# A column of 128 maxima is turned by a second VectorE transpose and stored as four rows of 32

## The chip, the cores and the metric

The kernel runs on one core of a Trainium2 chip. The metric is the device time of one execution in microseconds (us), taken as the median over several executions. The engines are named as the profile names them: PE is TensorE's matmul (PEld its weight load), DVE is VectorE, ACT is ScalarE, POOL is GpSimd, and SPq is the queue of SyncE, from which nearly all transfers are issued.

## The reference

Two branches of the same input x (2048 rows of 512) are computed and mixed by a gate. Branch a is attention with 32 query heads of width 16 that share one key head and one value head; branch b is a feed-forward layer with SiLU. Everything is float32.

```python
def _A_ref(x, wq, wk, wv, wo):
    q = (x @ wq).reshape(B, S, H, Dh).transpose(0, 2, 1, 3)   # H = 32, Dh = 16
    k = x @ wk
    v = x @ wv
    scores = jnp.einsum("bhqd,bkd->bhqk", q, k) * (Dh ** -0.5)
    p = softmax(scores, axis=-1)
    o = jnp.einsum("bhqk,bkd->bhqd", p, v)
    return o.transpose(0, 2, 1, 3).reshape(B, S, H * Dh) @ wo
def _B_ref(x, w1, w2):
    h = silu(jnp.einsum("bsd,df->bsf", x, w1))                # 512 -> 1792
    return jnp.einsum("bsf,fd->bsd", h, w2)                   # 1792 -> 512
g = sigmoid((x * gate_w).sum(-1, keepdims=True))
out = g * _A_ref(x, wq, wk, wv, wo) + (1 - g) * _B_ref(x, w1, w2)
```

## The kernel before

Operands are split into two float16 parts with fixed scales, and each product is made of three float16 matmuls. The fixed scales hold only while the data lie in certain ranges. The kernel therefore works in two passes. The first pass computes the whole output with fixed scales and, on the side, collects maxima of its operands. At its end line 1461 reads `flag`, and a second pass with scales worked out from the data runs only if a maximum lay outside its range (`RANGES`).

After a short prologue the first pass is one long pipeline, `attention`. It goes through 32 rounds, one for each block of 512 query rows, block of 128 query columns (8 heads) and half of these heads. A round has 16 steps, one for each 128 keys. In a step PE writes scores into a PSUM tile `S` (line 1212, in eight matmuls of 32 rows), ACT turns them into exponentials `P` (line 1218, 128x1024 at a time, two of them a step), DVE takes the lower half of `P`'s mantissa into a float16 tile `L` (line 1237), and PE adds value sums from `P` and `L` (line 1316). Between these, PE does the matmuls of the feed-forward layer, of the next queries and of the output projection (line 869). At the end of a round DVE takes the sums out of PSUM by two transposes (lines 1137 and 1138), and POOL and DVE finish them.

The instructions of each engine stand in an order that a planner in the kernel wrote out when it was built. It keeps its own estimates of when each engine is free (`pe`, `act`, `dve`, `pool`), and counts PE's instructions in blocks of 256, of which each takes at least `BLOCK` = 3.65 us by its estimate. On the chip each engine keeps to its order and waits for semaphores.

SPq's queue is in order as well. At the start of each round `load_q` (lines 268 to 272) issues eight loads from DRAM into the query buffer `qb` that the next round uses, in rows of 1 KB. They wait until PE is through with the last use of that buffer.

The collected maxima are small DVE work, the `chores`, which the planner puts where it believes DVE to be free. Each `absmax` leaves a column of `mxs` (128 x 32). Once all query blocks are done, `gather` runs: it adds the last column (lines 694 and 695), turns `mxs` in blocks of 32 x 32 (line 696, the result in `mt`, columns 0 to 31 of the buffer `raw`), takes the maximum of each row (line 697, into `mr`, column 32 of the same buffer) and stores the 128 maxima into a small DRAM tile `md` (line 698). `row` loads `md` back as one row on one partition (line 703), `check` compares it with `RANGES` (lines 709 to 714), and `verdict` writes `flag` (lines 717 to 719).

Of the kernel before, what the change touches and what calls it, by code (L numbers as in the profile page):

```python
# [47 lines left out]
def kernel(  # L48
# [21 lines left out]
    nc = tc.nc  # L70
# [35 lines left out]
    raw_ = [consts.tile([128, 512], F32, name=f"raw{n}") for n in range(2)]  # L106
# [7 lines left out]
    md = dram.tile([128], F32, name="md")  # L114
# [21 lines left out]
    def absmax(dst, src, axis=AX.X):  # L136
        nc.vector.tensor_reduce(dst, src, axis=axis, op=OP.max, apply_absolute_value=True)
# [539 lines left out]
    def chores():  # L677

        todo = []
        for kt in range(KD):  # L680
            for h in range(2):
                todo.append(lambda kt=kt, h=h: absmax(mxs[:, M_X + 2 * kt + h:M_X + 2 * kt + h + 1], xs[:, 0, kt, h * S // 2:(h + 1) * S // 2]))
                todo.append(lambda kt=kt, h=h: absmax(mxs[:, M_1 + 2 * kt + h:M_1 + 2 * kt + h + 1], w1s[:, 0, kt, h * F // 2:(h + 1) * F // 2]))
        for f in range(0, FT_ALL, 2):
            todo.append(lambda f=f: absmax(mxs[:, M_2 + f // 2:M_2 + f // 2 + 1], flat(w2s[:, 0, f:f + 2])))
        for o in range(0, NO, 2):
            todo.append(lambda o=o: absmax(mxs[:, M_O + o // 2:M_O + o // 2 + 1], flat(wo_s[:, 0, o:o + 2])))

        todo.append(lambda: absmax(mxs[:, M_Q:M_Q + 1], flat(wqs[:, 0])))
        todo.append(lambda: absmax(mxs[:, M_VV:M_VV + 1], VF[:, :, 0:16], AX.XY))  # L690

        def gather():
            mt, mr = raw_[0][:, 0:32], raw_[0][:, 32:33]
            nc.vector.tensor_reduce(mr[0:64], um, axis=AX.X, op=OP.min)
            nc.vector.tensor_scalar(mxs[0:64, M_B:M_B + 1], mr[0:64], -1.0, SHIFT * LAM / ONE, op0=OP.mult, op1=OP.add)
            nc.vector.transpose(mt, mxs)
            nc.vector.tensor_reduce(mr, mt, axis=AX.X, op=OP.max)
            nc.sync.dma_start(md.rearrange("(p o) -> p o", o=1), mr)

        m, m1 = raw_[1][0:1, 0:128], raw_[1][0:1, 128:160]  # L700

        def row():
            nc.sync.dma_start(m, md.rearrange("(o p) -> o p", o=1))

        g = raw_[1][0:1, 160:160 + 4 * len(RANGES)].rearrange("p (a b) -> p a b", a=4)

        def check(n0):
            if n0 == 0:
                nc.vector.tensor_reduce(m1, m.rearrange("p (a b) -> p b a", a=4), axis=AX.X, op=OP.max)
            for n in range(n0, min(n0 + 3, len(RANGES))):  # L710
                a, b, lo, hi = RANGES[n]
                nc.vector.tensor_reduce(g[:, 0, n:n + 1], m1[:, a:b], axis=AX.X, op=OP.max)
                nc.vector.tensor_scalar(g[:, 1, n:n + 1], g[:, 0, n:n + 1], lo, None, op0=OP.is_lt)
                nc.vector.tensor_scalar(g[:, 2, n:n + 1], g[:, 0, n:n + 1], hi, None, op0=OP.is_gt)

        def verdict():
            nc.vector.tensor_tensor(g[:, 3], g[:, 1], g[:, 2], op=OP.max)
            nc.vector.tensor_reduce(g[:, 0, 0:1], g[:, 3], axis=AX.X, op=OP.max)
            nc.vector.tensor_copy(flag, g[:, 0, 0:1])

        return todo, gather, row, *(lambda n=n: check(n) for n in range(0, len(RANGES), 3)), verdict


# [767 lines left out]
```

## Time and profile before

| | us |
|---|---|
| median of three executions | 1073.58 (1071.99 to 1075.55) |
| the profiled execution, its own time | 1073.73 |
| its span, first to last instruction | 1071.9 |
| the time around the span | 1.8 |
| `md` is stored (SPq, line 698) at | 753.64 |
| `md` is loaded back (SPq, line 703) at | 762.71 |

In what follows a row of the groups reads: line, engine, operation, what it writes and reads, how many, busy time. A row of the timeline reads: start in the span, duration, engine and operation, how many were merged, and in square brackets the engine's idle time before it with what ended that. A row of the waits reads: who waited for whom, time in total, how many times, the longest. A row of the stages reads: the stretch, its length, busy time and number of instructions of PE, PEld, DVE, ACT and POOL, then the clock that TensorE was granted as a share of the full one, the share of the 16 DMA engines that was busy, and GB/s.

### The profile page before, as it was taken

Reading aid. Unit: us, or ns where it says so; the run is one execution under the profiler, and the core shown is the slowest. Engines: PE = TensorE matmul, PEld = TensorE weight load, DVE = VectorE, ACT = ScalarE, POOL = GpSimd, SP = SyncE. Lnnn points to the kernel's source line nnn. Section 1 sums busy time; section 2 is a strip of 40 time slices with the busy share of each in tenths; the row PEclk is TensorE's granted clock in tenths of the full one; section 3 lists DMA queues with packets and bytes.
Section 4 is the critical chain, followed back from the end, with each engine's and each line's share of the span. In section 5 each row is a group of like instructions: output and inputs, shape, how many; then the busy total and the mean of one; then the engine's idle time right before and its main releaser. Section 6 shows DMA issues by size and latency. Waiting matters only on the chain.

```text
span 1071.9 us, 65095 instructions
## 1 busy us (share of the span) xinstructions
PE 1019.1 (95%) x30622; PEld 565.9 (53%) x30622; DVE 909.3 (85%) x823; ACT 1000.5 (93%) x1116; POOL 470.9 (44%) x396
## 2 busy tenths in 40 slices
PE   8999999899999999999999999999899999999997
PEld 5445555455555555555555555555445555545553
DVE  6699889999999778888887888888788798888886
ACT  6899999999999999999999999999899999999990
POOL 2035326634252464344742436266344266644641
PEclk9999999999999999999999999999999999999999
DMA  7321111100000100000000010000000000000001
GB/s 255 89 66 56 55 56 55 31 11 22 12 21 15 40 22 12 22 12 21 5 22 12 12 60 12 21 6 21 12 11 11 10 26 31 12 11 12 4 4 43
DMA packets 23783, 32.90 MB, mean 31 GB/s; under 512 B 5121, under 2 KB 13474, under 8 KB 23506
## 3 DMA queue, kind: packets, MB, share of 16 engines
q1 hardware_dynamic: 22978, 28.49, 8.5%
q8 instruction: 241, 3.95, 1.5%
q14 instruction: 36, 0.29, 0.1%
q0 software_dynamic: 96, 0.10, 0.0%
q10 hardware_dynamic: 432, 0.07, 0.0%
HBM read 20.12 MB, written 8.52 MB: 27 GB/s over the span
## 4 chain that ended last, share of the span: by engine, by line
PE 37%; DVE 23%; ACT 22%; issue 8%; POOL 8%; DMA 1%; SPq 0%; DVEq 0%; ACTq 0%; POOLq 0%
ACT P L1218 20%; DVE L L1237 14%; PE pm L869 13%; PE pv L1316 12%; PE S L1212 8%; POOL T L1143 2%; ACT e L883 2%; POOL U L1145 2%; POOL U L1150 2%; PE S L873 1%; POOL T L1146 1%; PE pm L873 1%; DVE e L888 1%; DVE U L1138 1%; DVE w2s L203 1%
## 5 line engine op out<-in xcount | busy, mean ns | idle before, releaser
L1218 ACT ACTIVATE P<-S 128x1024 f32<-128x1024 f32 x1024 | 963.2, 1070 | 32.3 <-PE S L1212 27.7
L1237 DVE TENSOR_TENSOR L<-P 128x2048 f16<-128x2048 f32 x240 | 599.3, 2514 | 27.7 <-ACT P L1218 27.0
L1212 PE MATMUL S<-qb,KT 50*32 50x512 f16 x8192 | 438.1, 380 | 13.8 <-ACT P L1218 11.3
L1212 PEld LDWEIGHTS <-KT 50*32 50x32 f16 x8192 | 188.8, 90 | 232.1 <-issue 149.7
L1316 PE MATMUL pv<-P,VF 64*32 64x512 f32 (+1 forms) x5552 | 306.6, 499 | 0.0
L869 PE MATMUL pm<-w2s,H 64*32 64x512 f16 x4800 | 255.0, 377 | 4.7 <-issue 2.7
L869 PE MATMUL pm<-xs,w1s 64*32 64x512 f16 x5376 | 254.4, 376 | 4.7 <-DVE e L888 3.4
L1143 POOL TENSOR_TENSOR T<-T,U 128x512 f32<-128x512 f32 x31 | 84.5, 2725 | 287.1 <-DVE U L1138 287.1
L890 POOL CAST H<-e 128x512 f16<-128x512 f32 x56 | 54.4, 971 | 215.5 <-DVE e L888 215.5
L869 PEld LDWEIGHTS <-w1s 64*32 64x32 f16 x5376 | 109.0, 93 | 60.5 <-issue 17.8
L869 PEld LDWEIGHTS <-H 64*32 64x32 f16 x4800 | 108.5, 93 | 49.9 <-issue 9.8
L1316 PEld LDWEIGHTS pv<-P,VF 64*32 64x32 f32 x5552 | 109.2, 106 | 39.7 <-issue 7.4
L1316 PE MATMUL pv<-L,VP 64*32 64x512 f16 x1904 | 102.6, 377 | 10.4 <-DVE L L1237 10.1
L1316 PE MATMUL pv<-P,VP 64*32 64x512 bf16 x1904 | 106.5, 388 | 1.4 <-DVE T L1137 0.9
L891 POOL TENSOR_TENSOR H<-e,H 128x512 f16<-128x512 f32 x56 | 103.6, 1850 | 4.5
L1316 PEld LDWEIGHTS <-VP 64*32 64x32 f16 x3808 | 69.1, 93 | 56.4 <-issue 31.5
L869 PE MATMUL pm<-xs,wqs 64*32 64x512 f16 x1152 | 85.0, 375 | 0.8 <-DVE e L888 0.6
L888 DVE SCALAR_TENSOR_TENSOR e<-e,pm 128x512 f32<-128x512 f32 x56 | 38.1, 681 | 42.3 <-ACT e L883 42.3
L1150 POOL TENSOR_TENSOR U<-U 128x48 f32<-128x48 f32 (+1 forms) x62 | 69.8, 1126 | 2.4
L869 PE MATMUL pm<-wo_s,O 64*32 64x512 f16 x1440 | 67.5, 375 | 1.2 <-DVE acc L843 0.8
L1145 POOL TENSOR_TENSOR U<-T,mu 128x96 f32<-128x96 f32 x31 | 47.6, 1535 | 2.4
L843 DVE SCALAR_TENSOR_TENSOR acc<-pm,g,acc 128x512 f32<-128x512 f32 x42 | 31.3, 745 | 16.1 <-PE pm L869 15.3
(180 smaller groups left out, 608.0 us busy)
## 6 DMA issues: line engine op xcount, KB each, us to landing
qb<-qd SPq DMA_DIRECT2D x189, 32.0 KB
raw<-in_B_w_dram SPq DMA_DIRECT2D x22, 256.0 KB
xn<-in_A_x_dram SPq DMA_DIRECT2D x8, 512.0 KB
out_dram<-acc SPq DMA_DIRECT2D x16, 256.0 KB
qd<-qx SPq DMA_DIRECT2D x12, 256.0 KB
w1r<-in_B_w_dram SPq DMA_DIRECT2D x2, 512.0 KB
raw<-in_A_wo_dram SPq DMA_DIRECT2D x4, 256.0 KB
qb<-sh SPq DMA_DIRECT2D x62, 2.0 KB
```

Of the source, the lines that this page charges most:

```text
L843: nc.vector.scalar_tensor_tensor(a, po, gate[:, n:n + 1], a, op0=OP.mult, op1=OP.add)
L869: nc.tensor.matmul(self.bank[32 * m:32 * m + 32], l(i, rows, 32 * m), r(j, rows), start=first, stop=last)
L888: nc.vector.scalar_tensor_tensor(e, e, 1.0, ph, op0=OP.add, op1=OP.mult)
L890: nc.gpsimd.tensor_copy(H[:, 0], e)
L891: nc.gpsimd.tensor_tensor(H[:, 1], e, H[:, 0], op=OP.subtract)
L1143: eng.tensor_tensor(T, T, U, op=OP.add)
L1145: eng.tensor_tensor(z[:, :, 1:1 + DIGITS], T3[:, :, 17:17 + DIGITS], mu[:, :, 1:].to_broadcast([128, 16, DIGITS]), op=OP.mult)
L1150: eng.tensor_tensor(first, first, second, op=OP.add)
L1212: nc.tensor.matmul(sc[32 * m:32 * m + 32, f], KT[b:b + 50, k0:k0 + 32], qtile[i][b:b + 50, j], start=True, stop=True)
L1218: nc.scalar.activation(P[:, 2 * j:2 * j + 2], sc, AF.Exp, scale=scale_of(c, o))
L1237: nc.vector.tensor_tensor(L[s], P, upper(P), op=OP.subtract)
L1316: nc.tensor.matmul(pvs[i][h][32 * j:32 * j + 32, cols], a[r], b[r, j, cols], start=start, stop=rest == n)
```

## The change

In `gather` the maxima stand in column 32 of `raw`, one on each of 128 partitions. After the change a second DVE transpose reads columns 32 to 63 of `raw` and writes columns 0 to 31. It turns each block of 32 x 32, so the 32 maxima of partitions 0 to 31 become row 0 of the result, those of 32 to 63 row 32, and so on; the other rows hold what lay in columns 33 to 63 and are not used. The store takes rows 0, 32, 64 and 96, 32 values each, instead of 128 single values. The bytes in `md` are the same, and so is all that reads them.

```diff
             nc.vector.transpose(mt, mxs)
             nc.vector.tensor_reduce(mr, mt, axis=AX.X, op=OP.max)
-            nc.sync.dma_start(md.rearrange("(p o) -> p o", o=1), mr)
+            nc.vector.transpose(mt, raw_[0][:, 32:64])
+            nc.sync.dma_start(md.rearrange("(p n) -> p n", p=4), mt[0:128:32])
```

The instructions of PE, ACT and POOL stand in the same order as before. Lines behind 698 have a number that is higher by one after the change.

DVE around `gather`, before (`raw_79` is the buffer that holds `mt` and `mr`):

```order
L694 TENSOR_REDUCE raw_79<-um 64x1 [waits DVE_49]
L695 TENSOR_SCALAR mxs<-raw_79 64x1 [waits DVE_49]
L696 STREAM_TRANSPOSE raw_79<-mxs 128x32 [waits DVE_49]
L697 TENSOR_REDUCE raw_79<-raw_79 128x1 [waits DVE_49]
L1237 TENSOR_TENSOR L<-P 128x2048 [waits Activation_49]
```

DVE at the same place, after:

```order
L694 TENSOR_REDUCE raw_79<-um 64x1 [waits DVE_49]
L695 TENSOR_SCALAR mxs<-raw_79 64x1 [waits DVE_49]
L696 STREAM_TRANSPOSE raw_79<-mxs 128x32 [waits DVE_49]
L697 TENSOR_REDUCE raw_79<-raw_79 128x1 [waits DVE_49]
L698 STREAM_TRANSPOSE raw_79<-raw_79 128x32 [waits DVE_49]
L1238 TENSOR_TENSOR L<-P 128x2048 [waits Activation_49]
```

One transpose stands between the last reduction and the next `L`, and it waits for the reduction before it on the same engine.

SPq around the store, as a difference of the two kernels (`sh` is a small DRAM tile of query shifts, `qd` the queries in DRAM):

```order
 L396 DMA sh_3_114<-e 4x512 [waits DMAHW2_49,DVE_49]
 L396 DMA sh_3_114<-e 4x512 [waits DMAHW3_49]
-L698 DMA md<-raw_79 128x1 [waits DMAHW4_49,DVE_49]
+L699 DMA md<-raw_79 4x32 [waits DMAHW4_49,DVE_49]
 L268 DMA qb_81<-qd_3_89 16x2x512 [waits DMAHW5_49,PE_49]
 L269 DMA qb_81<-qd_3_89 16x2x512 [waits DMAHW6_49]
```

The store keeps its place in the queue and its waits; only its shape is another.

## The prediction

> **What bounds the kernel now.** I read the page first, then the list of waits, then the stages and the timeline around the store of `md`, and last the transfers there.
>
> ```profile
> span 1071.9 us, 65095 instructions
> PE 1019.1 (95%) x30622; PEld 565.9 (53%) x30622; DVE 909.3 (85%) x823; ACT 1000.5 (93%) x1116; POOL 470.9 (44%) x396
> ```
>
> PE and ACT are both nearly full, DVE less so. Work on DVE or SPq costs time only where PE or ACT waits for it; and a gap in which both PE and ACT stand still is lost for good, since neither has 5% to spare.
>
> ```profile
> engine line waited for: us in total, times, longest us
> ACT P L1218 <- PE S L1212: 27.7, 45, 3.5
> PE S L1212 <- ACT P L1218: 11.3, 23, 1.0
> PE pv L1316 <- DVE L L1237: 10.1, 21, 1.2
> PE pm L869 <- issue: 2.9, 2, 2.7
> ```
>
> Over the whole run PE and ACT wait for each other in pieces of about half a microsecond. One piece stands out: PE stood for 2.7 us with "issue" named, that is, with nothing the profile shows to wait for, and the longest wait of ACT for PE is 3.5 us. The stages and the chain show where both are.
>
> ```profile
> 755.00:760.00 5.00, 4.06 (x141) 2.08 (x126) 5.00 (x4) 4.79 (x6) 0.00 (x0) 1.00 0.13 21
> 760.00:765.00 5.00, 3.24 (x72) 1.47 (x79) 1.68 (x1) 1.07 (x2) 0.00 (x0) 0.66 0.11 26
> 765.00:770.00 5.00, 4.21 (x147) 2.14 (x139) 4.54 (x4) 5.00 (x6) 3.00 (x2) 1.00 0.02 5
> 758.42 0.64 PE pm L869 x21
> 759.06 2.70 issue
> 761.76 1.04 PE pm L869 x9
> 763.32 1.02 ACT L1218 ACTIVATE P<-S 128x1024 f32<-128x1024 f32 x1 [3.53 <-PE S L1212]
> 764.95 2.85 ACT L1218 ACTIVATE P<-S 128x1024 f32<-128x1024 f32 x3 [0.61 <-PE S L1212]
> ```
>
> The first three rows are stages, the next three the chain of work that ended last, the last two ACT's timeline. Between 760 and 765 us ACT worked for 1.07 of 5 us. The gap of PE lies on the chain, and after it the granted clock of the stage is 0.66: of 5 us, (1 - 0.66) x 5 / 0.5 = 3.4 us passed at half speed.
>
> Why did PE stand? It had no instructions, and the transfers tell why. The rows are, in this order: the issues of the whole run that bear on it, with their sizes; the store of `md` on SPq and loads of `qb` behind it; the packets of 754.3 to 754.9 us; the fetches of instructions in the whole run, and those in 756 to 757 us, in 726 to 727.5 us and in 792 to 794 us.
>
> ```profile
> qb<-qd SPq DMA_DIRECT2D x189, 32.0 KB
> md<-raw SPq DMA_DIRECT2D x1, 0.5 KB
> ...
> 753.64 0.34 SPq L698 DMA_DIRECT2D md<-raw  x1
> 754.97 0.32 SPq L268 DMA_DIRECT2D qb<-qd  x1
> 756.92 4.23 SPq L268 DMA_DIRECT2D qb<-qd  x1
> ...
> DMA packets 144, 0.00 MB, mean 1 GB/s; under 512 B 144, under 2 KB 144, under 8 KB 144
> ...
> q8 instruction: 241, 3.95, 1.5%
> ...
> q8 instruction: 1, 0.02, 28.5%
> ...
> q8 instruction: 1, 0.02, 3.6%
> ...
> q8 instruction: 1, 0.02, 3.1%
> ```
>
> The 144 packets are the store of `md`: 128 single values of 4 bytes and 16 more. Shares are of 16 engines, so the 241 fetches took 0.015 x 16 x 1071.9 / 241 = 1.07 us each on average, and the one of 756 to 757 us took 0.285 x 16 x 1 = 4.56 us. Having begun between 756 and 757 it ended between 760.6 and 761.6, and PE went on at 761.76. One issue of a load on SPq was held in the same stretch, from 756.92 to 761.15. The two later rows are fetches that fell among loads of `qb` as well, without a store of `md` before them: 0.036 x 16 x 1.5 = 0.86 us and 0.031 x 16 x 2 = 0.99 us. So the loads alone do not hold a fetch; what is particular here is the scatter of 128 small writes some 2 us earlier. That it is the cause is inferred from the order in time, in one execution.
>
> **The change, part by part.** *The added transpose.* These are DVE's rows at the place.
>
> ```profile
> 753.18 0.21 DVE L696 STREAM_TRANSPOSE raw<-mxs 128x32 f32<-128x32 f32 x1
> 753.43 0.19 DVE L697 TENSOR_REDUCE raw<-raw 128x1 f32<-128x32 f32 x1
> 754.33 2.29 DVE L1237 TENSOR_TENSOR L<-P 128x2048 f16<-128x2048 f32 x1 [0.71 <-ACT P L1218]
> ```
>
> One transpose of the same shape takes 0.21 us, and the step from its end to the next instruction (753.39 to 753.43) another 0.04: 0.25 us. Behind it DVE waits 0.71 us for ACT's `P`, so 0.46 us of that cover is left, and the cost on the path is 0. If the cover were gone, `L` would come 0.25 us later, and with it PE's sums (line 1316); that is the upper end. A gain from it is excluded, for nothing is taken off DVE.
>
> *The store.* It leaves 0.25 us later, at 753.89. Behind it on SPq is the load at 754.97, which waits for PE's last use of the buffer; from the end of the store's issue (753.98, then 754.23) 0.74 us are left. Cost 0. The reader of `md`, at 762.71 on SPq, is later by far; and should the held issue at 756.92 shrink from 4.23 to the 0.32 us of the row above it, the rest of the queue comes 3.9 us earlier. That by itself gains nothing, since these loads fill the buffer of the next round, and the end of this round, the transpose of line 1137, is at 765.47 us with the next one 33 us on:
>
> ```profile
> 728.58 0.71 DVE L1137 STREAM_TRANSPOSE T<-pv 128x512 f32<-128x512 f32 x1
> 765.47 0.72 DVE L1137 STREAM_TRANSPOSE T<-pv 128x512 f32<-128x512 f32 x1 [3.79 <-PE pv L1316]
> 798.51 0.69 DVE L1137 STREAM_TRANSPOSE T<-pv 128x512 f32<-128x512 f32 x1
> ```
>
> *The writes.* 128 writes become 4, of 128 bytes each, and the same number of bytes. The trace has no store of that shape, so its hold is bounded. If the hold goes by the number of writes, the estimate from the rows above is (761 - 754.6) / 128 = 0.05 us for one and 0.2 us for four, over before the fetch of 756 to 757 us begins; even counted as sixteen pieces of 32 bytes it is 0.8 us, over by 755.7. If it goes by the transfer and not by its writes, the fetch is held as before and nothing is gained. I take the first, as nearest to the rows: the run has 189 loads of `qb` on the same queue, in rows of 1 KB, and the list of waits shows no second gap of PE of that kind (2.9 us in 2 times, 2.7 of them here).
>
> *What the gap is worth.* On PE: 2.70 us of standing, and half of the time at half speed with work to do, from 761.76 to about 764.8: 1.5 us. Sum 4.2 us. On ACT: 3.53 + 0.61 = 4.14 us idle, of which perhaps 0.2 would stay, since PE needs some work between two `S` in any case. Both come to about 4.1, and both engines lose it together, so that it isn't made up elsewhere. What is late next, once the gap is gone, is ACT: behind 765 it runs without a wait for PE. As a cross-check, the round that holds the gap took 765.47 - 728.58 = 36.9 us and the next 33.0.
>
> [...]
>
> *Sum.* 1073.73 (the profiled execution) - 4.15 + 0 + 0 = 1069.6. The profiled execution lies 0.15 above the median shown, so against the median it is 1069.4, or 0.39% less.
>
> **The rivals.** *A. As summed:* 1069.4.
>
> *B. A second slow stretch goes with the first.* One round later the clock drops once more:
>
> ```profile
> core 0: 1071.9 us, clock 0.995
> ...
> 795.00:800.00 5.00, 3.08 (x84) 1.23 (x73) 4.89 (x13) 4.72 (x6) 0.66 (x2) 0.89 0.04 10
> 800.00:805.00 5.00, 5.00 (x135) 2.30 (x123) 4.43 (x3) 3.16 (x4) 4.92 (x4) 0.77 0.01 3
> 800.97 1.03 ACT L1218 ACTIVATE P<-S 128x1024 f32<-128x1024 f32 x1 [1.25 <-PE S L1212]
> 802.81 3.94 ACT L1218 ACTIVATE P<-S 128x1024 f32<-128x1024 f32 x4 [0.82 <-PE S L1212]
> ```
>
> PE was busy for only 3.08 of 5 us, then the clock was 0.77 in the next stage, and ACT idled 1.25 + 0.82 = 2.07 us. If this drop depends on when the thin stretch falls, moving all by 4 us may undo it: 1069.4 - 2.1 = 1067.3. For it speaks that the round's end, where this thin stretch stands, comes 32 times, yet the mean clock of 0.995 leaves only 0.005 x 1071.9 / 0.5 = 10.7 us at half speed in the whole run, of which these two drops hold some 7; against it, that nothing in the thin stretch itself is changed.
>
> [...]
>
> *C. The scatter isn't the cause, or four rows hold the fetch as well.* Then 1073.6, with at most 0.25 on top. For it: the slow fetch is one event in one execution, and by the trace 2 us lie between the writes and the fetch. Against: it is the only gap of its kind, and the only scatter of its kind.
>
> *D. Half of it.* The fetch is held for less, say 2.7 us, and PE stands for about 1 us with no drop of the clock, or the clock drops at another thin stretch: 2 of 4 us are gained, 1071.5.
>
> *E. Slower.* The hold goes by the bytes that one DMA engine has to write: if the 4 rows go to 4 engines, each has 128 bytes instead of 8 values of 4, four times as much. The excess of the fetch, 4.56 - 1.07 = 3.5 us, would become 14 and the time about 1084. It decides if the fetch meets one of these engines. Against it: the many loads in rows of 1 KB, which hold no fetch for long (0.86 and 0.99 us above).
>
> **How the numbers follow.** What a measurement of this kernel can tell from no change is about 0.3%, or 3.2 us. Chances: A 0.52, B 0.20, C 0.14, D 0.10, E 0.04. Three executions spread over 3.6 us, so I give each case about 1.2 us to either side. Faster by over 0.3% means under 1070.4: A four times in five (0.42), nearly all of B (0.20), a quarter of D (0.03) and a trace of C: 0.66. Slower means over 1076.8: E and a trace of C, 0.05. The rest, 0.29, is within 0.3%. The range reaches down to 1066.5, which takes in most of B, and up to 1073.5, which takes in D and about half of C; what is left out is E, half of C and the lower end of B, under 2 in 10.
>
> **What would show it.** Right: no row "PE pm L869 <- issue" above 0.3 us, the fetch behind the store near 1 us, the issue of the load behind it near 0.35 us, no wait of ACT for PE over 2 us near 760, clock 1.00 in the stage of 760 to 765, one more transpose of 0.2 us on DVE in front of a shorter wait for `P`. Wrong: a fetch of over 3 us at the same place (C or E), or a gap of the same kind elsewhere, which would say that the hold comes from something other than this store.

## The result, and the profile after

The changed kernel takes 1069.91 us (median of seven executions, 1068.91 to 1071.30) against 1073.58 (median of seven, 1071.99 to 1075.55): a ratio of 0.9965, 95% interval 0.9953 to 0.9977. It is 3.7 us faster. The profiled execution took 1069.22 us, of them 1067.3 in the span. In the rows below the score matmul is line 1213, the exponential 1219, `L` 1238, the store of `md` 699.

The page's first rows, and the list of waits of the whole run:

```profile
span 1067.3 us, 65096 instructions
PE 1017.0 (95%) x30622; PEld 567.2 (53%) x30622; DVE 908.4 (85%) x824; ACT 1000.3 (94%) x1116; POOL 470.9 (44%) x396
...
ACT P L1219 <- PE S L1213: 23.1, 42, 1.7
PE S L1213 <- ACT P L1219: 11.3, 23, 1.0
PE pv L1317 <- DVE L L1238: 9.5, 20, 1.2
```

The row in which PE waited 2.9 us for "issue" is gone, and the longest wait of ACT for PE is 1.7 us instead of 3.5. ACT's total wait for PE fell by 4.6 us, which is what the span lost (1071.9 to 1067.3). The stages around the store, and ACT's and DVE's timelines there:

```profile
755.00:760.00 5.00, 5.00 (x183) 2.71 (x175) 5.00 (x4) 4.85 (x6) 0.00 (x0) 1.00 0.20 46
760.00:765.00 5.00, 4.20 (x147) 2.13 (x132) 5.00 (x5) 5.00 (x6) 2.21 (x2) 1.00 0.02 5
...
759.61 13.86 ACT L1219 ACTIVATE P<-S 128x1024 f32<-128x1024 f32 x15 [0.15 <-PE S L1213]
...
753.09 0.19 DVE L697 TENSOR_REDUCE raw<-raw 128x1 f32<-128x32 f32 x1
753.31 0.21 DVE L698 STREAM_TRANSPOSE raw<-raw 128x32 f32<-128x32 f32 x1
753.99 2.29 DVE L1238 TENSOR_TENSOR L<-P 128x2048 f16<-128x2048 f32 x1 [0.46 <-ACT P L1219]
```

ACT works through all of 760 to 765 us (5.00 of 5 us, 1.07 before), the clock of that stage is 1.00 instead of 0.66, and ACT's idle time there is 0.15 us instead of 3.53 + 0.61. The added transpose takes 0.21 us and DVE's wait for `P` behind it shrank from 0.71 to 0.46. The store on SPq and two of the loads behind it, the packets of 754 to 755.5 us, and the fetch of instructions in 755.5 to 757.5:

```profile
753.55 0.56 SPq L699 DMA_DIRECT2D md<-raw  x1
754.63 0.33 SPq L268 DMA_DIRECT2D qb<-qd  x1
756.61 1.16 SPq L268 DMA_DIRECT2D qb<-qd  x1
...
DMA packets 8, 0.00 MB, mean 0 GB/s; under 512 B 8, under 2 KB 8, under 8 KB 8
...
q8 instruction: 1, 0.02, 4.0%
```

8 packets instead of 144, and the fetch takes 0.04 x 16 x 2 = 1.28 us instead of 4.56. The issue of the load at the same place (756.61, before 756.92) takes 1.16 us instead of 4.23. The ends of the rounds:

```profile
728.24 0.71 DVE L1138 STREAM_TRANSPOSE T<-pv 128x512 f32<-128x512 f32 x1
761.26 0.71 DVE L1138 STREAM_TRANSPOSE T<-pv 128x512 f32<-128x512 f32 x1
794.09 0.69 DVE L1138 STREAM_TRANSPOSE T<-pv 128x512 f32<-128x512 f32 x1
```

The round that held the gap is 33.0 us long, from 36.9, which is 3.9 us; the next is 32.8, from 33.0. Of the 4.6 us between the two spans 0.3 was there before 728 us and some 0.4 came after 765.

### The profile page after: what moved, and what is told of

It is laid out like the page before. It is cut to its first block, busy times and chain, and to the rows that moved or that the text cites. A ratio compares the mean times of both kernels' runs of the same rounds, so it can differ in the third digit from the quotient of the medians.

```text
span 1067.3 us, 65096 instructions
## 1 busy us (share of the span) xinstructions
PE 1017.0 (95%) x30622; PEld 567.2 (53%) x30622; DVE 908.4 (85%) x824; ACT 1000.3 (94%) x1116; POOL 470.9 (44%) x396
## 4 chain that ended last, share of the span: by engine, by line
PE 34%; ACT 24%; DVE 22%; POOL 9%; issue 9%; DMA 1%; ACTq 0%; DVEq 0%; POOLq 0%
ACT P L1219 22%; DVE L L1238 14%; PE pm L870 11%; PE pv L1317 11%; PE S L1213 8%; POOL T L1144 3%; POOL U L1146 2%; POOL T L1147 2%; ACT e L884 2%; POOL U L1151 1%; PE S L874 1%; DVE U L1139 1%; PE pm L874 1%; DVE e L889 1%; DVE T L1138 1%
## 5 line engine op out<-in xcount | busy, mean ns | idle before, releaser
L870 PE MATMUL pm<-w2s,H 64*32 64x512 f16 x4800 | 251.4, 375 | 3.0 <-DVE acc L844 1.1
L1151 POOL TENSOR_TENSOR U<-U 128x48 f32<-128x48 f32 (+1 forms) x62 | 65.9, 1062 | 2.4
```

Of the source, the lines that this page charges most:

```text
L870: nc.tensor.matmul(self.bank[32 * m:32 * m + 32], l(i, rows, 32 * m), r(j, rows), start=first, stop=last)
L1151: eng.tensor_tensor(first, first, second, op=OP.add)
```

## Experiments

Two theories stood against each other. The first is that of the prediction: the 128 single values hold a fetch of PE's instructions, and the transpose costs nothing. The second is chance: the slow fetch of the profile was one event in one execution, and the gain came with the transpose or with the 0.25 us by which it moves the store.

### The transpose alone

```diff
+            nc.vector.transpose(mt, raw_[0][:, 32:64])
             nc.sync.dma_start(md.rearrange("(p o) -> p o", o=1), mr)
```

> The second transpose is kept, but its result is not used: the column is stored as 128 single values, as before. Theory (the scatter of 4-byte writes holds a fetch of PE's instructions, the transpose costs nothing): 1073.6 us, the time of before, with a fetch of over 3 us and a gap of PE of 2 to 3 us behind the store, and a transpose of 0.2 us under DVE's wait for P. Rival (the slow fetch was chance, or the gain came with the transpose and the 0.25 us by which it moves the store): 1070 us and no such fetch.

Measured: 1073.27 us, ratio 1.000 to before (0.9987 to 1.0012). The transpose is there, the gain is not. The profile of this kernel, first PE's row in the list of waits, then SPq, DVE and ACT in the timeline, then the fetches in 755 to 757 and in 761 to 763 us:

```profile
PE pm L870 <- issue: 1.5, 1, 1.5
...
754.07 0.34 SPq L699 DMA_DIRECT2D md<-raw  x1
755.77 3.44 SPq L269 DMA_DIRECT2D qb<-qd  x1
...
754.75 2.29 DVE L1238 TENSOR_TENSOR L<-P 128x2048 f16<-128x2048 f32 x1 [0.46 <-ACT P L1219]
...
762.67 13.91 ACT L1219 ACTIVATE P<-S 128x1024 f32<-128x1024 f32 x15 [2.45 <-PE S L1213]
...
q8 instruction: 1, 0.02, 9.5%
...
q8 instruction: 1, 0.02, 10.1%
```

The fetch behind the store is slow again (0.095 x 16 x 2 = 3.04 us), and so is the next one (3.23 us), which begins only some 8 us after the store. DVE's wait of 0.46 us is that of the changed kernel, so the transpose is hidden, as summed. In this execution the gap was smaller than in the profile of before: PE stood for 1.5 us, ACT for 2.45, and the clock did not drop there.

### No DRAM at all

```diff
-            nc.sync.dma_start(md.rearrange("(p n) -> p n", p=4), mt[0:128:32])
+            nc.sync.dma_start(m.rearrange("o (p n) -> o p n", p=4), mt[0:128:32])
...
-            nc.sync.dma_start(m, md.rearrange("(o p) -> o p", o=1))
```

> The four rows go straight into the row on one partition, from SBUF to SBUF; the store to DRAM and the load back are left out. Theory: no small write to DRAM is left and none was held by the four rows, so the time is that of the changed kernel, 1069.9 us within 1 us. Rival (four rows of 128 bytes still hold something): up to 1 us faster than it, with shorter transfers behind the store.

Measured: 1069.39 us, ratio 0.9965 to before (0.995 to 0.998), the same as the changed kernel. So the four rows of 128 bytes cost nothing that this measurement can see (its interval is some 3 us wide), and no gain is left at this place that it could show.

### Thirteen stores instead of one

Behind every second of the first 26 chores a column of maxima is copied into a free column of `raw`, and from there, in all but the control, moved by one more transfer. What the kernel computes is unchanged.

```diff
+        def with_store(f, n):
+            def both():
+                f()
+                src = raw_[0][:, 64 + 32 * n:65 + 32 * n]
+                nc.vector.tensor_copy(src, mxs[:, 0:1])
+                nc.sync.dma_start(to_[n].rearrange("(p o) -> p o", o=1), src)   # not in the control
+            return both
+        todo = [with_store(f, q // 2) if q % 2 == 0 and q < 32 - 6 else f for q, f in enumerate(todo)]
```

> The changed kernel, with 13 small DVE copies of a column of maxima behind every second of the first 26 chores, and no store. It is the control for the next kernels. Both theories: 1070 us, at most 13 x 0.15 = 2 us more.

> The control, and each of the 13 copies is also stored into DRAM of its own as 128 single values side by side, as the kernel before stores its column. Theory (such a store holds a fetch that comes within some 2 to 6 us behind it): PE fetches instructions every 4 us or so, so that most of the 13 stores meet one: 7 to 13 fetches of over 3 us, and up to 13 x 4.1 us, 1098 to 1123 us. Rival (chance): 1070 us, fetches of 1 us.

Measured: the control 1069.92 us (ratio 0.9969, 0.9957 to 0.9982), the 13 scatters 1110.80 us (1.0351, 1.0333 to 1.0368). The 13 stores cost 40.9 us, 3.1 us each. Read packet by packet, the control has one fetch over 1.8 us in the whole run, of 1.83, and none over it among these stores; the 13 scatters have 13, of 2.7 to 3.9 us. PE's rows in the list of waits of the 13 scatters (its lines stand 11 higher than in the changed kernel), and one of its fetches, in 219 to 220 us, where it is the only packet:

```profile
PE pm L881 <- issue: 13.2, 8, 3.4
PE S L1224 <- issue: 6.1, 5, 2.2
PE pv L1328 <- issue: 3.4, 2, 2.6
...
DMA packets 1, 0.02 MB, mean 16 GB/s; under 512 B 0, under 2 KB 0, under 8 KB 0
q8 instruction: 1, 0.02, 22.1%
```

The fetch took 0.221 x 16 = 3.5 us, with no load of `qb` near it. PE stood for 22.7 us in 15 gaps of the same kind; the rest of the 41 us lies in part in the granted clock, which dropped to half six times between 205 and 385 us, for 3.4 us each, against none in the control. In the kernel before such a drop reads 0.50, from 761.35 to 764.76 us. At that half speed 3.4 us lose at most 1.7 us of work, so the six drops account for some 10 us at most. Chance is excluded: 13 slow fetches among 13 stores, and none in the control. It isn't one fetch for each store, though. Behind the store issued at 269.58 us one fetch begins at once, before the store's packets move, and the next, at 277.93, is as fast as any; behind the last store, at 368.67, two fetches are slow.

### What about the store holds the fetch

Each of the next kernels changes the 13 transfers, and two of them, m3 and m7, also the width of the copy before each. The lines below are shortened; the expectations behind them stand in the order m2 to m9.

```diff
 to_: 13 DRAM tiles [128]
-                nc.sync.dma_start(to_[n].rearrange("(p o) -> p o", o=1), src)
+                nc.sync.dma_start(to_[n][:, 0:1], src)                    # m2: to_ is [128, 128]; m6: [128, 16]
+                nc.sync.dma_start(to_[n], src)                            # m3: to_ [128, 32] from 32 columns; m7: [128, 8] from 8
+                nc.sync.dma_start(raw_[1][:, 256 + n:257 + n], src)       # m4: SBUF
+                nc.sync.dma_start(to_[n].rearrange("(p o) -> p o", o=1), src[0:32])   # m5: to_ is [32]; m8: src[0:4], [4]
+                nc.sync.dma_start(src, gate_w[128:256].rearrange("(p o) -> p o", o=1)) # m9: a load
```

> As the 13 scatters, but each of the 128 values goes to the start of a DRAM row of its own, 512 bytes apart. If the hold comes from 128 writes falling on one place of 512 bytes in DRAM (each waits for the one before it): 1070 to 1073 us, no fetch over 2 us. If it goes by the number of writes of 4 bytes, wherever they fall: 1110.8 us as with the 13 scatters, 13 slow fetches.

> As the 13 scatters, but each of the 128 partitions stores a row of 128 bytes, side by side (16 KB a store; the copy is 128x32). If the number of writes or of packets decides: 1110 us or more, 13 slow fetches. If it is the writes of 4 bytes that share a place: 1070 to 1074 us. If a store of many rows under 512 bytes holds in proportion to its bytes, 32 times those of the scatter: far above 1110.

> As the 13 scatters, but the 128 single values go to another column in SBUF. If DRAM's side of the write is what holds: 1070 to 1072 us, no fetch over 2 us. If 128 packets of 4 bytes are enough wherever they go: 1110.8 us, 13 slow fetches.

> As the 13 scatters, but each stores only 32 of the 128 values, side by side in 128 bytes. By the estimate of 0.05 us a write the hold is 1.6 us, over before most fetches or hidden by PE's lead: 1070 to 1076 us, with fetches of 1 to 2.5 us. If the hold goes by the transfer and not by its writes: 1110.8 us.

> As the 13 scatters, but each value has 64 bytes of its own, so that 8 of them share 512 bytes and the store covers 8 KB. If it is the sharing of 512 bytes that holds: 1085 to 1110 us, 13 fetches of over 2.5 us. If only values within the same 64 bytes wait for each other: 1070 to 1072 us, no fetch over 2 us.

> 128 rows of 32 bytes side by side (4 KB a store), so that 16 rows share 512 bytes and 2 share 64. If sharing 512 bytes holds: as with the 13 scatters or less, 1085 to 1110 us. If sharing within 64 bytes holds, by how many share: 2 writes instead of 16, a hold of under 0.8 us, 1070 to 1073 us. If only writes narrower than 32 bytes hold: 1070 to 1072 us as well.

> Four single values side by side (16 bytes), from four partitions. The 32 values gave slow fetches of 3 to 4 us, not the 1.6 us that the estimate of 0.05 us a write gives, so the hold doesn't go by the count alone. If it goes by the transfer, as soon as neighbours come from different partitions: 1085 to 1095 us with 12 or 13 slow fetches. If by how many writes share a place: 4 instead of 16 or more, under 1 us a store, 1070 to 1073 us.

> The same 13 places, but each transfer loads 128 single values that lie side by side in DRAM into a column in SBUF. If it is writing to a shared place that holds: 1070 to 1072 us, no fetch over 2 us. If reads of 4 bytes from one place wait for each other as well: 1085 to 1110 us and 13 slow fetches.

| 13 transfers of | us, median | ratio to before (95%) | fetches over 2.5 us |
|---|---|---|---|
| m0: none (the control) | 1069.92 | 0.9969 (0.9957 to 0.9982) | 0 |
| m1: 128 x 4 bytes, side by side | 1110.80 | 1.0351 (1.0333 to 1.0368) | 13 |
| m5: 32 x 4 bytes, side by side | 1091.54 | 1.0158 (1.0138 to 1.0178) | 12 |
| m8: 4 x 4 bytes, side by side | 1070.25 | 0.9958 (0.9942 to 0.9975) | 0 |
| m6: 128 x 4 bytes, 64 bytes apart | 1070.26 | 0.9954 (0.9937 to 0.9970) | 0 |
| m2: 128 x 4 bytes, 512 bytes apart | 1070.08 | 0.9970 (0.9954 to 0.9985) | 0 |
| m7: 128 rows of 32 bytes, side by side | 1070.96 | 0.9967 (0.9955 to 0.9980) | 0 |
| m3: 128 rows of 128 bytes, side by side | 1071.47 | 0.9978 (0.9969 to 0.9988) | 0 |
| m4: 128 x 4 bytes, into SBUF | 1069.77 | 0.9965 (0.9953 to 0.9978) | 0 |
| m9: 128 x 4 bytes, loaded from DRAM | 1070.06 | 0.9959 (0.9945 to 0.9973) | 0 |

The last column is counted packet by packet. The kernels ran in three groups, each with its own runs of before, so the ratios are what is to be compared across them. The same stretch of the run, 205 to 380 us, reads in the control, the 13 scatters, the 32 values and the four values:

```profile
205.00:380.00 175.00, 172.13 (x5334) 95.62 (x5326) 159.22 (x144) 172.06 (x189) 67.30 (x59) 1.00 0.07 21
```

```profile
205.00:380.00 175.00, 150.23 (x4242) 85.88 (x4228) 130.05 (x120) 137.21 (x150) 57.85 (x51) 0.94 0.07 13
```

```profile
205.00:380.00 175.00, 155.69 (x4692) 86.24 (x4684) 139.89 (x128) 151.67 (x165) 60.11 (x53) 0.99 0.08 14
```

```profile
205.00:380.00 175.00, 172.08 (x5333) 95.83 (x5318) 159.25 (x144) 172.03 (x189) 67.00 (x59) 1.00 0.07 21
```

In 175 us the control and the four values finish 189 of ACT's instructions, the 13 scatters 150 and the 32 values 165.

What follows. It isn't the number of packets: 128 single values cost nothing when each has 64 bytes of its own (ratio 0.9954, the control 0.9969), or when they go to SBUF (0.9965). It isn't that the rows are short: rows of 32 and of 128 bytes cost nothing that is clear of the control (0.9967 and 0.9978). It isn't reading (0.9959). What is left is many narrow writes that fall side by side in DRAM. The runs show that such writes can be dear, 3.1 us for a store of 128, but not what happens at one of them, and the size alone doesn't decide it, since values 64 bytes apart are as narrow and free.

The estimate of 0.05 us a write fell: 32 values gave fetches of 3.0 to 4.0 us, no shorter than the 2.7 to 3.9 of 128. Two fetches, each the only packet of its stretch, one of the 32 values in 256 to 257 us and one of the values 64 bytes apart in 218.5 to 219.5 us, and behind them the packets of the store of `md` in the kernel before, in 754.3 to 754.9 us:

```profile
q8 instruction: 1, 0.02, 24.7%
...
q8 instruction: 1, 0.02, 8.5%
...
q1 hardware_dynamic: 144, 0.00, 12.9%
```

The fetches took 0.247 x 16 = 4.0 us and 0.085 x 16 = 1.4 us. The last row shows why the estimate fell: the 144 packets of the store took 0.129 x 16 x 0.6 / 144 = 0.009 us each, and all were over before 754.9, while the slow fetch began only behind 756. What holds it is not the time of the packets, but something that lasts longer than they do. Read packet by packet, in the four profiles with such stores (before, the transpose alone, 13 scatters, 32 values) all fetches that began 1.2 to 7.2 us behind the issue of one were slow, over 2.5 us. Of the three that began 8.0 us behind the nearest one was slow, and of those that began later none.

What 128 and 32 values have in common is the number of values that share 64 bytes, sixteen; four values, and rows of 32 bytes, of which two share 64, held nothing. So the hold might go by how many writes fall on one piece of DRAM. That fits which of the ten rows were slow, but it isn't shown: the number per piece wasn't varied by itself, four values may be free because they are few in all, rows of 32 bytes because they are wider, and the tiles also lie at other addresses. The size of the piece is bracketed only by the runs at 64 bytes apart and side by side.

The 128 values cost 3.1 us each and the 32 only 1.6 (the difference of the ratios, 0.0189 x 1073.5 / 13), with fetches of the same length. Part of that is the clock: at 0.94 against 0.99 in the stretch above, (1 - 0.94) x 175 / 0.5 = 21 us passed at half speed against 3.5, which is worth up to 9 us. PE also stood longer, 22.7 us against 18.1. The profiled spans are 1109.0 and 1092.9 us, 16 us apart, so these two cover most of it. Which DMA engine a fetch shares with the store isn't in these profiles.

## Why the prediction was right

It forecast 1069.4 us in a range of 1066.5 to 1073.5; 1069.91 were measured, and of its cases it was A.

- *The cause.* Inferred from order in time in one execution, and confirmed: with the transpose and the scatter the time is that of before, with 13 scatters there are 13 slow fetches. Rival C, chance, is out.
- *The added transpose at 0.* Right: 0.21 us as costed, 0.46 us of the wait left as worked out, and a time of 1073.27 when it stands alone.
- *The store that leaves 0.25 us later, and the loads behind it, at 0.* Right in effect: the load behind the store waits as before, and the gain is accounted for without what was saved on SPq, which no run tried by itself. The one sign that missed is here: the issue of the load behind the store was to come near 0.35 us and took 1.16, from 4.23. That the store's own issue takes 0.56 us instead of 0.34 was not in the sum; it is hidden as well.
- *The gap at 4.15 us.* Slightly too large: the round that held it lost 3.9 us, and the medians differ by 3.7. Part of the term is the clock, 1.5 us (0.50 from 761.35 to 764.76 us), and that part is not in every execution, as the profile with the transpose and the scatter shows (a gap of 1.5 us on PE, 2.45 on ACT, no drop of the clock there). The term was read from one execution in which both parts were full. The argument that neither engine has 5% to spare was a little off, since ACT at 93% has 7%; but that the gap isn't made up elsewhere came true, with 3.9 us of it lost in that round.
- *The writes.* Four rows hold nothing, as taken, and the run without DRAM shows that none of it was left. But the reason given, a hold by the number of writes at 0.05 us each, was wrong: 128 rows of 128 bytes were as free as four, and 32 single values held fetches as long as 128. That four rows were enough was in this sense luck, the right choice for a reason that didn't hold. The estimate also had the hold over by 761; with the transpose and the scatter a fetch that began some 8 us after the store was slow too (3.23 us).
- *Rival B.* The second drop of the clock is gone from this profile, as it allowed, but it was worth far less than the 2.1 us put on it:

```profile
790.00:795.00 5.00, 3.10 (x97) 1.49 (x82) 4.89 (x13) 5.00 (x7) 1.12 (x1) 1.00 0.08 17
795.00:800.00 5.00, 4.79 (x152) 3.10 (x158) 5.00 (x4) 4.06 (x5) 4.46 (x3) 1.00 0.01 3
796.13 8.74 ACT L1219 ACTIVATE P<-S 128x1024 f32<-128x1024 f32 x9 [0.83 <-PE S L1213]
805.73 1.03 ACT L1219 ACTIVATE P<-S 128x1024 f32<-128x1024 f32 x1 [0.86 <-PE S L1213]
```

  The clock is 1.00 and ACT still waits 0.83 + 0.86 us there, against 1.25 + 0.82, which leaves 0.4 us for the drop. The mistake was to count all of ACT's idle time in that stretch as the price of the clock. The drop also isn't tied to the change: the profiles with the transpose and the scatter, without DRAM, of four values, of values 512 bytes apart and into SBUF have one that begins at 794 to 798 us. So its absence from the profile of the changed kernel may be chance.
- *Rivals D and E.* D, half of the gap, and E, a hold by bytes, did not come. E's rule is refuted by the rows of 128 bytes: 32 times the bytes, no slow fetch.

## What to carry to other kernels

In these runs a transfer that nobody waits for stopped an engine, by a delay of the fetch of that engine's instructions, for up to some 8 us behind it. In the list of waits this showed as a long "issue" on PE (2.7 us), and in the list of transfers as one instruction fetch several times as long as the others (4.56 us, 1.07 on average). Look for a store of a column of single values just ahead of it: turn the column into a few rows before it is stored (here a transpose of 0.2 us gained 3.7), or give each value 64 bytes of its own, which was free in these runs (ratio 0.9954, against 0.9969 with no such store).

## What the runs showed of the hardware

The narrow stores delayed the fetches of another queue: they took 2.7 to 4.6 us instead of about 1 (1.07 on average in the kernel before), although they carry instructions and the store data. They delayed their own queue as well: between 205 and 385 us 10 packets of loads in rows of 1 KB took over 1 us with the 13 scatters, up to 2.8, and none over 0.4 in the control. How a store on one queue holds a fetch on another was not shown: no view here shows the DMA engines one by one. That 32 values held a fetch as long as 128, up to 4.0 us against 3.9, was not expected; that 64 bytes between values left no slow fetch was one of two cases named beforehand.
